# Two attention blocks on one core: a weight block loaded in two halves around the first key group, the last weight chunks in another order, a shorter head-by-head finish, and more products ahead of the first scores

## The chip, the cores and the metric

The kernel runs on one core of one Trainium2 chip. The metric is the device time of one execution in microseconds. Each comparison gives the median of the runs of a kernel, and a ratio to the kernel before, run on the same chip in the same rounds, with a 95% interval. The span of a profile was 1.7 to 1.9 us shorter than the device time of the same run.

## The reference

Two independent problems, A and B, of the same shape; their outputs are put side by side in the last dimension.

```python
B, Sq, D = 16, 32, 1024;  Hq, Hkv, Sk, Dh = 32, 4, 512, 128      # all bfloat16
q = (x @ wq).reshape(B, Sq, Hq, Dh).transpose(0, 2, 1, 3)
k, v = repeat(k_cache, 8, axis=1), repeat(v_cache, 8, axis=1)
p = softmax(einsum("bhqd,bhkd->bhqk", q, k) * Dh ** -0.5)
o = einsum("bhqk,bhkd->bhqd", p, v)
y = o.transpose(0, 2, 1, 3).reshape(B, Sq, Hq * Dh) @ wo          # (16, 32, 1024)
```

## The kernel before

The contraction of the q projection has 8 chunks of 128 (`DC = 8`, `HC = 4`). The first eight heads of A are projected chunk by chunk while their weights arrive (`w0`, `first_heads`). Everything after that is one long stream of products of 512 columns (the other projections, then the output projections). 128 attention slots are woven into it: each has four score matmuls, one exponential on ScalarE, sums on VectorE and, five slots later, four value matmuls. The loads go through one queue, that of the sync engine; in the trace of before, the loads from chunk 4 (landed at 10.35 us) to the first V group (29.98 us) landed in the order of their issue.

```python
            load_x(0, 0, TT // 2)                  # input, transposed later on TensorE
            load_w0(0, 1, 0, NF // 2)              # weights: chunk 0, heads 0 to 2
            load_x(0, TT // 2, TT)
            load_w0(0, 1, NF // 2, NF)             # chunk 0, heads 3 to 5
            load_w0(1, 2, 0, NF)                   # chunk 1
            load_x(2, 0, TT)
            load_w0(2, 3, 0, NF)
            load_w0(3, 4, 0, NF)
            load_w0(0, HC, NF, REP)                # chunks 0 to 3, heads 6 and 7
            load_w0(HC, HC + 1, 0, REP)            # chunk 4, all eight heads
            load_x_transposed(HC)                  # input chunks 4 and 5, transposed by DMA
            load_w0(HC + 1, HC + 2, 0, REP)        # chunk 5
            load_w0(HC + 2, DC, 0, REP)            # chunks 6 and 7
            load_x_transposed(HC + 2)              # input chunks 6 and 7
            load_wq(0, 2)                          # third weight block: heads 8 to 11, 1 MB
            load_k(0)                              # first K group, four transposed loads of 128 KB
            load_wq(0, 3)
            load_k(1)
            load_v(0)                              # first V group, 512 KB
            # ... (cut)
            warm_up(22)                            # 26 matmuls on constants in all
            # ... (cut: chunks 0 to 3)
            first_heads(range(REP), range(HC, DC - 2))
            for n, h in enumerate((0, 2, 4, 1, 5, 3, 6, 7)):
                first_heads((h,), (DC - 2, DC - 1))
                copy = nc.vector.tensor_copy if n % 2 else nc.scalar.copy
                copy(out=qT[0, 0][:, :, h, :], in_=first_q[h].rearrange("p (b s) -> p b s", s=SQ))
            # ... (cut)
            units = stream()
            run(units, 5)                          # five products of head 8 ahead of the first scores
            # ... (cut: plan of the later loads)
            for i in range(total_slots + LAG):
                if live:
                    do_loads(i)
                    scores(i)
                run(units, 1)
                # ... (cut: sums)
                if i >= LAG:
                    values(i - LAG)
                # ... (cut)
                run(units, 5)
                # ... (cut)
                run(units, 1 - (i % 4 == 3))
```

## Time and profile before

| | before |
|---|---|
| device time, median of 3 runs | 343.95 us (343.72 to 345.05) |
| span of the profiled run | 342.3 us |
| PE busy | 99% |
| PE start to start, 512 columns, full rate | 0.216 us |
| wait before the third weight block | 0.38 us |
| first product of chunk 4 to last matmul | 326.25 us |

The last row is worked out from the start times of the matmuls in the trace (12.682 us and 338.933 us).

The busy times of the engines, from the page of the kernel before (PE is TensorE's matmuls, PEld its weight loads, DVE VectorE, ACT ScalarE, POOL GpSimd; us, share of the span, instructions):

```profile
PE 337.9 (99%) x2128; PEld 214.1 (63%) x2128; DVE 266.2 (78%) x336; ACT 185.9 (54%) x209; POOL 46.7 (14%) x206
```

The waits of PE's weight loads between 5 and 60 us, kernel before (engine, line, what it waited for: us in total, times, longest us):

```profile
PEld L533 <- DMA w_sb<-in_A_wq_dram: 0.8, 2, 0.6
PEld L302 <- DMA wq_sb<-in_A_wq_dram: 0.7, 1, 0.7
PEld L523 <- DMA x_sb<-in_A_x_dram: 0.2, 1, 0.2
```

The timeline of the kernel before around the first scores (start, duration, engine, line, operation, output and inputs, count; in brackets the idle time before and what ended it; a row holds only what falls into the window that was asked for):

```profile
18.08 1.67 PE L533 MATMUL q_ps<-xT,w_sb 128*128 128x512 bf16 x7
...
19.79 0.69 DVE L561 CAST qT<-q_ps 128x512 bf16<-128x512 f32 x1 [0.17 <-PE q_ps L533]
...
19.96 0.76 PEld L302 LDWEIGHTS <-wq_sb 128*128 128x128 bf16 x5 [0.71 <-DMA wq_sb<-in_A_wq_dram]
19.97 1.25 PE L302 MATMUL q_ps<-xT,wq_sb 128*128 128x512 bf16 x5 [0.21 <-ACT qT L561]
...
21.05 0.60 PE L358 MATMUL s_ps<-qT,kT 128*128 128x256 bf16 x4
```

PE is the bound. What can be won without removing matmuls is the time in which PE stands still. The last matmul of the first eight heads starts at 19.372 us and the next is due 0.216 us later, at 19.59; it starts at 19.97. Two waits stand on this gap: the weight load waits for the third block (DMA), and the matmul is put down to a copy of ScalarE. The load landed at 19.92 us.

### The profile page before, as it was taken

What the parts mean: (1) busy time and instruction counts of PE and PEld (TensorE: products, weight loads), DVE (VectorE), ACT (ScalarE), POOL (GpSimd) and SP (SyncE); (2) the same over time, 40 slices, a digit from 0 to 9 for tenths busy, and PEclk for the clock granted to TensorE, in tenths of its full rate; (3) what the DMA queues carried; (4) which work ended last, traced back from release to release, by engine and by line L of the source; (5) the groups of instructions that cost most, each with busy time, mean ns of one, the idle gap of its engine ahead of it and who ended that gap; (6) DMA issues with size and microseconds to landing.
All of it is one profiled execution on the core that took longest, in us unless ns stands there. A gap on an engine that the chain in (4) does not pass through costs nothing.

```text
span 342.3 us, 5511 instructions
## 1 busy us (share of the span) xinstructions
PE 337.9 (99%) x2128; PEld 214.1 (63%) x2128; DVE 266.2 (78%) x336; ACT 185.9 (54%) x209; POOL 46.7 (14%) x206
## 2 busy tenths in 40 slices
PE   8999999999999999999999999999999999999996
PEld 6456666666666666666666666666666666666555
DVE  1057988888889888988888888888988888888540
ACT  3067666676676666666655455455455445555010
POOL 0001111100111111111101112222122110111100
PEclk9999999999999999999999999999999999999999
DMA  6999999999999999899999957999349995440001
GB/s 184 278 230 193 280 272 238 262 245 239 224 230 271 216 255 241 240 259 273 320 307 231 265 124 192 309 292 236 106 114 289 349 191 139 100 116 0 17 17 33
DMA packets 127088, 71.70 MB, mean 209 GB/s; under 512 B 75859, under 2 KB 126291, under 8 KB 127059
## 3 DMA queue, kind: packets, MB, share of 16 engines
q1 hardware_dynamic: 126528, 70.21, 86.0%
q0 software_dynamic: 384, 1.05, 1.2%
q8 instruction: 17, 0.28, 0.3%
q14 instruction: 15, 0.10, 0.1%
q10 hardware_dynamic: 144, 0.07, 0.1%
HBM read 50.86 MB, written 2.10 MB: 155 GB/s over the span
## 4 chain that ended last, share of the span: by engine, by line
PE 96%; DMA 1%; SPq 1%; ACT 0%; issue 0%; ACTq 0%
PE f_ps L321 32%; PE q_ps L302 28%; PE ob L426 16%; PE s_ps L358 16%; PE q_ps L533 3%; DMA w_sb<-in_A_wq_dram 1%; SPq L478 0%; SPq L466 0%; ACT qT L561 0%; ACT o_sb L330 0%; SPq L706 0%; ACTq L330 0%
## 5 line engine op out<-in xcount | busy, mean ns | idle before, releaser
L366 ACT ACTIVATE p_sb<-s_ps,shift 128x1024 bf16<-128x1024 f32 x128 | 142.6, 1114 | 100.5 <-PE s_ps L358 82.6
L377 DVE TRANSPOSE_TENSOR_REDUCE parts<-p_sb 128x32 f32<-128x1024 bf16 x128 | 158.8, 1241 | 20.0 <-ACT p_sb L366 18.3
L321 PE MATMUL f_ps<-wo_sb,oT 128*128 128x512 bf16 (+1 forms) x544 | 131.8, 367 | 0.0
L302 PE MATMUL q_ps<-xT,wq_sb 128*128 128x512 bf16 x448 | 117.6, 379 | 0.2 <-ACT qT L561 0.2
L426 PE MATMUL ob<-p_sb,v_sb 128*128 128x256 bf16 x512 | 76.8, 273 | 0.0
L358 PE MATMUL s_ps<-qT,kT 128*128 128x256 bf16 x512 | 76.8, 273 | 0.0
L321 PEld LDWEIGHTS <-oT 128*128 128x128 bf16 x544 | 53.2, 98 | 36.0
L358 PEld LDWEIGHTS <-kT 128*128 128x128 bf16 x512 | 56.9, 113 | 28.3
L302 PEld LDWEIGHTS <-wq_sb 128*128 128x128 bf16 x448 | 43.7, 98 | 32.0 <-DMA wq_sb<-in_A_wq_dram 0.7
L426 PEld LDWEIGHTS <-v_sb 128*128 128x128 bf16 x512 | 50.1, 98 | 20.0
L448 DVE TENSOR_TENSOR oT<-r,ob 128x512 bf16<-128x512 f32 x64 | 44.0, 687 | 22.6 <-PE ob L426 22.1
L412 DVE STREAM_TRANSPOSE r<-rall 128x512 f32<-128x512 f32 x64 | 44.2, 691 | 1.1
L310 ACT CAST qT<-q_ps 128x512 bf16<-128x512 f32 x56 | 32.6, 583 | 13.8 <-PE q_ps L302 13.8
L395 POOL COPY half<-cs 64x32 f32<-64x32 f32 x32 | 6.5, 204 | 228.4 <-DVE cs L385 228.4
L330 ACT CAST o_sb<-f_ps 128x512 bf16<-128x512 f32 (+1 forms) x17 | 9.5, 559 | 24.4 <-PE f_ps L321 16.7
L533 PE MATMUL q_ps<-xT,w_sb 128*128 128x512 bf16 (+1 forms) x70 | 15.1, 366 | 0.1
L385 DVE TENSOR_REDUCE cs<-parts 128x32 f32<-128x128 f32 x32 | 12.1, 377 | 1.1
L407 DVE RECIPROCAL rall<-sums 128x32 f32<-128x32 f32 x32 | 10.2, 318 | 1.6 <-POOL sums L404 1.6
L533 PEld LDWEIGHTS <-w_sb 128*128 128x128 bf16 x70 | 6.7, 99 | 7.2 <-DMA w_sb<-in_A_wq_dram 0.8
L561 DVE CAST qT<-q_ps 128x512 bf16<-128x512 f32 x4 | 2.8, 691 | 9.7 <-PE q_ps L533 9.6
L332 POOL DMA_DIRECT2D out_dram<-o_sb x8 | 4.6, 574 | 33.2 <-ACT o_sb L330 33.1
L396 POOL TENSOR_TENSOR half<-half,cs 64x32 f32<-64x32 f32 x32 | 7.8, 243 | 2.6
(25 smaller groups left out, 46.5 us busy)
## 6 DMA issues: line engine op xcount, KB each, us to landing
v_sb<-in_A_v_cache_dram SPq DMA_DIRECT2D x16, 512.0 KB, 6.8
wq_sb<-in_B_wq_dram SPq DMA_DIRECT2D x8, 1024.0 KB, 6.1
wo_sb<-in_A_wo_dram SPq DMA_DIRECT2D x8, 1024.0 KB, 6.9
v_sb<-in_B_v_cache_dram SPq DMA_DIRECT2D x16, 512.0 KB, 4.6
wo_sb<-in_B_wo_dram SPq DMA_DIRECT2D x8, 1024.0 KB, 8.6
wq_sb<-in_A_wq_dram SPq DMA_DIRECT2D x6, 1024.0 KB, 6.0
kT<-in_A_k_cache_dram SPq DMA_TRANSPOSE x64, 4.7
out_dram<-o_sb POOLq DMA_DIRECT2D x8, 128.0 KB, 4.2
```

The source lines that it names most:

```text
L302: nc.tensor.matmul(ps[:], lhsT=w[:, dc, (h % 4) * DH:(h % 4 + 1) * DH], rhs=xT[pr][:, dc, :], start=(dc == 0), stop=(dc == DC - 1),)
L310: nc.scalar.copy(out=qT[pr, g][:, :, hl, :], in_=ps[:].rearrange("p (b s) -> p b s", s=SQ),)
L321: nc.tensor.matmul(ps[:, 0:width], lhsT=oT[pr, tt][:, h, :], rhs=wo_tiles[pr, nh, h // REP][:, h % REP, off:off + width], start=(h == 0), ...
L358: nc.tensor.matmul(s_ps[:, c, :], lhsT=kT[:, i % GRP, c, :], rhs=qT[pr, g][:, b, :, :].rearrange("p h s -> p (h s)"), start=True, stop=True,)
L366: nc.scalar.activation(out=p_sb[:], in_=s_ps[:], func=ACTF.Exp, bias=shift[:], scale=SCALE)
L377: nc.vector.tensor_reduce(out=parts[k][:, q, :, :].rearrange("p c h -> p (c h)"), in_=st[i]["p"][:].rearrange("p c (h s) -> p (c h) s", s=SQ),
L385: nc.vector.tensor_reduce(out=cs[:], in_=parts.pop(k)[:].rearrange("p q c h -> p q h c"), axis=AX.X, op=ALU.add,)
L407: nc.vector.reciprocal(out=rall[:, k, :], in_=quad.pop(k)[:])
L412: nc.vector.transpose(out=r[:].rearrange("p n s -> p (n s)"), in_=rall[:, k, o * 2 * REP:(o + 1) * 2 * REP] .unsqueeze(2).to_broadcast([P, ...
L426: nc.tensor.matmul(ob[j][:, q, :], lhsT=v_sb[:, i % GRP, c, :], rhs=st[i]["p"][:, c, :], start=(c == 0), stop=(c == KC - 1),)
L448: nc.vector.tensor_tensor(out=out, in0=rcp.pop(j)[:].rearrange("p (q h) s -> p q h s", h=REP), in1=ob.pop(j)[:].rearrange("p q (h s) -> p ...
L533: nc.tensor.matmul(first_q[h][:, ts], lhsT=w0[dc // HC][:, dc % HC, h * DH:(h + 1) * DH], rhs=xT[0][:, dc, ts], start=(dc == 0 and t0 == 0 ...
```

## The change

Its intent is to take this gap away. The third block is loaded in two halves of two heads, one ahead of the first K group and one behind it. The last weight chunks come in another order. Only chunk 7 is finished head by head (before, chunks 6 and 7), which puts the eight copies closer together, so eight products of head 8 (before, five) are put ahead of the first scores to cover them. The input of B comes in two later loads instead of three, and some later weight loads are issued a slot earlier.

```diff
-            def load_wq(pr, c4, eng=None, parts=((0, 4),)):
+            def load_wq(pr, c4, a=0, b=4):          # loads heads a to b of a block of four
 ...
             load_x_transposed(HC)
-            load_w0(HC + 1, HC + 2, 0, REP)
-            load_w0(HC + 2, DC, 0, REP)
+            load_w0(HC + 1, DC - 1, 0, REP)
             load_x_transposed(HC + 2)
-            load_wq(0, 2)
+            load_w0(DC - 1, DC, 0, REP)
+            load_wq(0, 2, 0, 2)
             load_k(0)
+            load_wq(0, 2, 2, 4)
             load_wq(0, 3)
 ...
-            first_heads(range(REP), range(HC, DC - 2))
-            for n, h in enumerate((0, 2, 4, 1, 5, 3, 6, 7)):
-                first_heads((h,), (DC - 2, DC - 1))
+            first_heads(range(REP), range(HC, DC - 1))
+            for n, h in enumerate((0, 2, 4, 6, 5, 7, 1, 3)):
+                first_heads((h,), (DC - 1,))
 ...
-            run(units, 5)
+            run(units, DC)
 ...
-                need = ((c4 - 2) * 4 * DC - 5) / 6.75
+                need = ((c4 - 2) * 4 - 1) * DC / 6.75
 ...
-            for n, (d0, d1) in enumerate(((0, 2), (2, 5), (5, DC))):
-                at(GRP * (n + 3) - 2, load_xT_b, d0, d1)
+            for n in range(2):
+                at(GRP * (n + 3) - 2, load_xT_b, n * HC, (n + 1) * HC)
```

More of the change, by code (lines that the diff above doesn't have):

```diff
@@ L240, in fast_path @@
             wq_tiles, wo_tiles, k_tiles, v_tiles = {}, {}, {}, {}
-            def load_wq(pr, c4, eng=None, parts=((0, 4),)):
-                t = blk_tile([P, DC, 4 * DH], "wq_sb")
+            def load_wq(pr, c4, a=0, b=4):
+                if a == 0:
+                    wq_tiles[pr, c4] = blk_tile([P, DC, 4 * DH], "wq_sb")
                 v = problems[pr][3].rearrange("(c p) n -> p c n", p=P)
-                for a, b in parts:
-                    (eng or nc.sync).dma_start(
-                        out=t[:, :, a * DH:b * DH],
-                        in_=v[:, :, (c4 * 4 + a) * DH:(c4 * 4 + b) * DH],
-                    )
-                wq_tiles[pr, c4] = t
+                nc.sync.dma_start(
+                    out=wq_tiles[pr, c4][:, :, a * DH:b * DH],
+                    in_=v[:, :, (c4 * 4 + a) * DH:(c4 * 4 + b) * DH],
+                )
             def load_wo(pr, nh, hg):
```

## The prediction

> **What bounds the kernel.** TensorE. The page has PE busy 99% of a 342.3 us span at clock 1.0, and the chain of waits is 96% PE. In steady state one slot repeats every 2.385 us, and 512-column matmuls start 0.216 us apart [...]. Summing the matmuls after 4.06 us at these rates gives about 332.5 us of the 335.2 us up to the last one, so no reordering can win more than a little. The waits on PE and its weight loads show where it stands still: 0.29 us before chunk 2 (8.06 to 8.35, weights landing at 8.31), and 0.38 us before the first product of the third weight block (previous one due to end at 19.59, next starts 19.97; its 1 MB load landed at 19.92). Between 20 and 339 us PE waits for nothing on record.
>
> **What the change does.** No matmul, copy or byte is added or removed.
> 1. The third weight block is split: the half for heads 8 and 9 (512 KB) ahead of the first K group, the rest behind it. Loads land one after the other at about 250 to 285 GB/s here, so the first half should land about 2 us earlier, near 17.7 to 18 us, and the first K groups near 18.5 to 20 instead of 20.4 to 22.0. The 0.38 us gap goes. The second half should land near 22 and is needed near 24.
> 2. Chunk 5 now loads together with chunk 6 (512 KB): it lands about 1 us later, near 13.4, and is needed at 14.4. Chunk 7 lands near 15.5, needed at 17.9. No new wait expected.
> 3. Only chunk 7 is finished head by head, so eight products take 1.73 us instead of 3.45, and the eight copies to SBUF bunch up. VectorE's four copies of 0.69 us start near 18.5 and end near 21.1 to 21.3 (before: 20.48). The first scores need all eight. The eight products of head 8 (1.73 us, before only five) fill this time: scores are due at 21.3. It just fits; I allow 0.05 us, at worst 0.2, of new wait.
> 4. The stream is three products ahead: three fewer in the tail (0.65 us), three more in front: neutral. The B input comes in two transposed loads instead of three and some weight loads issue a slot earlier; both have slack.
>
> **Net.** 0.38 us removed, about 0.05 to 0.1 added: 0.3 us, all on the critical path, 0.1% of the span. The 0.29 us gap before chunk 2 stays.
>
> **Predicted time:** 343.65 us, 8 in 10 between 343.1 and 344.3. The runs of before spread from 343.72 to 345.05, more than the effect. Chances: faster by over 2% 0.005, within 2% 0.99, slower 0.005.
>
> **What would show it.** Right: no weight-load wait on the third block's load; first product of head 8 starts near 19.6, first scores near 21.3 to 21.45 with eight products ahead (before, 21.055 with five, which equals 21.70 with eight); the tail's run of output products is three shorter; span near 342.0. Step 3 wrong: PE or its sequencer waits for the VectorE copy before the first scores by over 0.2 us. Step 2 wrong: a wait for weights at 14.4 or 16.1.
>
> **What would make it wrong.** Split loads with 512-byte rows being slower, the second half or the first values' load arriving late (the latter's margin is 1.2 us now), the transposed loads' slow issue (1.3 to 3.8 us each on the queue) delaying what is behind them, or a shift of three products making ScalarE or VectorE late in some slot of the steady state, which repeats 128 times.

## The result, and the profile after

| | before | after |
|---|---|---|
| device time, median of 6 runs each | 344.01 us (343.72 to 345.05) | 343.94 us (343.29 to 344.54) |
| span of the profiled run | 342.3 us | 342.1 us |
| wait before the third weight block | 0.38 us | none |
| first product of chunk 4 | 12.68 us | 12.88 us |
| first product of chunk 4 to last matmul | 326.25 us | 325.86 us |

The ratio is 0.9991, with an interval from 0.9974 to 1.0008. A ratio is the mean time of one kernel's fast runs over that of the other's in the same rounds, so it is not quite the ratio of the medians above. The interval holds 1: the times do not show a gain.

The busy times of the changed kernel, from its page:

```profile
PE 338.1 (99%) x2128; PEld 214.6 (63%) x2128; DVE 265.6 (78%) x336; ACT 185.7 (54%) x209; POOL 46.6 (14%) x206
```

The view of the waits of PE lists one entry for the whole of the changed kernel, the start of the program. That of its weight loads between 5 and 60 us has none. The timeline around the first scores:

```profile
18.05 1.89 PE L533 MATMUL q_ps<-xT,w_sb 128*128 128x512 bf16 x8
...
18.47 2.05 ACT L561 CAST qT<-q_ps 128x512 bf16<-128x512 f32 x4 [9.58 <-PE q_ps L533]
...
18.69 2.48 DVE L561 CAST qT<-q_ps 128x512 bf16<-128x512 f32 x4 [10.18 <-PE q_ps L533]
19.57 1.61 PEld L301 LDWEIGHTS <-wq_sb 128*128 128x128 bf16 x8
...
19.78 1.89 PE L301 MATMUL q_ps<-xT,wq_sb 128*128 128x512 bf16 x8
21.29 0.55 PEld L357 LDWEIGHTS <-kT 128*128 128x128 bf16 x4
21.51 0.60 PE L357 MATMUL s_ps<-qT,kT 128*128 128x256 bf16 x4
```

The PE rows now follow one another without brackets. The bracket on the copies is idle time of ScalarE and VectorE, which cost PE nothing here: VectorE's four copies end at 21.17 us (18.69 + 2.48) and the scores start at 21.51, when they were due. The same matmul after the scores starts 0.387 us earlier, counted from chunk 4, and this difference stays the same to within 0.01 us to the end of the kernel. The tail shows the three products moved to the front, with the chain of waits of the kernel before first:

```profile
325.53 13.69 PE f_ps L321 x95
```

and that of the changed kernel:

```profile
325.98 13.04 PE f_ps L320 x92
```

But the span fell by only 0.2 us. The rest was lost before chunk 4, where both kernels issue the same loads and matmuls. The early PE rows of the timeline, kernel before, and the wait of its weight loads before chunk 2:

```profile
5.24 2.11 PE L533 MATMUL q_ps<-xT,w_sb 128*128 128x256 bf16 x13
7.18 0.61 PE L523 MATMUL xT_ps<-ident,x_sb 128*128 128x128 bf16 x8
...
8.35 10.91 PEld L533 LDWEIGHTS <-w_sb 128*128 128x128 bf16 x52 [0.62 <-DMA w_sb<-in_A_wq_dram]
```

and changed kernel:

```profile
5.25 2.58 PE L533 MATMUL q_ps<-xT,w_sb 128*128 128x256 bf16 x13
7.66 0.61 PE L523 MATMUL xT_ps<-ident,x_sb 128*128 128x128 bf16 x8
```

The same 13 matmuls took 0.47 us longer. In the trace the first 256-column matmuls start 0.213 us apart, and from some moment on 0.109 us apart. This moment was 5.2 us in the trace of before and 6.5 us in that of after. Matmuls of 128 columns show the switch too: they start 0.107 us apart before it and 0.056 us after it. It falls differently from run to run (3.7 to 7.0 us, table below); what sets its moment is not shown. The granted clock in these two profiles reads 1.00 all the time, so the switch has to be read from the start times. In the kernel before PE then stood 0.29 us for the weights of chunk 2, which landed at 8.31 us; in the changed kernel they landed at 7.54 us, and PE stood 0.02 us. So each trace has one early loss of its own, and the two partly cancel: chunk 4 starts 0.19 us later in the changed kernel, and 0.387 - 0.193 = 0.194 us is what its last matmul is early.

### The profile page after: what moved, and what is told of

The parts are those of the page before. It is cut to its first block, busy times and chain, and to the rows that moved or that the text cites. A ratio compares the mean times of both kernels' runs of the same rounds, so it can differ in the third digit from the quotient of the medians.

```text
span 342.1 us, 5510 instructions
## 1 busy us (share of the span) xinstructions
PE 338.1 (99%) x2128; PEld 214.6 (63%) x2128; DVE 265.6 (78%) x336; ACT 185.7 (54%) x209; POOL 46.6 (14%) x206
## 4 chain that ended last, share of the span: by engine, by line
PE 99%; ACT 0%; issue 0%; ACTq 0%
PE f_ps L320 32%; PE q_ps L301 28%; PE ob L425 16%; PE s_ps L357 16%; PE q_ps L533 4%; PE q_ps L515 1%; PE xT_ps L523 0%; ACT o_sb L329 0%; ACTq L329 0%
## 5 line engine op out<-in xcount | busy, mean ns | idle before, releaser
L309 ACT CAST qT<-q_ps 128x512 bf16<-128x512 f32 x56 | 32.6, 583 | 15.4 <-PE q_ps L301 15.4
L533 PE MATMUL q_ps<-xT,w_sb 128*128 128x512 bf16 (+1 forms) x70 | 15.4, 377 | 0.0
```

Source lines behind the costliest of these rows:

```text
L309: nc.scalar.copy(out=qT[pr, g][:, :, hl, :], in_=ps[:].rearrange("p (b s) -> p b s", s=SQ),)
L533: nc.tensor.matmul(first_q[h][:, ts], lhsT=w0[dc // HC][:, dc % HC, h * DH:(h + 1) * DH], rhs=xT[0][:, dc, ts], start=(dc == 0 and t0 == 0 ...
```

## The experiments

All twelve runs gave correct outputs. e11 is not in the table; its trace lacks records, and it is told in its section. The table collects the traces. "Full rate" is when the half rate ends, read from the start times to about 0.1 us. "Block" is the landing of the weights for the first product of the third block and when PE was due for it, "V" the same for the first V group; a wait is in brackets. "Interval" runs from the first product of chunk 4 to the last matmul.

| trace | full rate | chunk 4 | block landed / due | V landed / due | interval | ratio to before (95%) |
|---|---|---|---|---|---|---|
| before | 5.2 | 12.68 | 19.92 / 19.59 (0.38) | 29.98 / 31.23 | 326.25 | |
| after | 6.5 | 12.88 | 17.50 / 19.78 | 30.79 / 31.68 | 325.86 | 0.9991 (0.9974 to 1.0008) |
| e1_split_alone | 5.6 | 12.58 | 18.09 / 19.49 | 31.51 / 30.74 (0.81) | 326.70 | 1.0030 (1.0001 to 1.0058) |
| e2_whole_block | 7.0 | 13.12 | 18.69 / 20.02 | 28.81 / 31.93 | 325.86 | 1.0001 (0.9977 to 1.0025) |
| e3_five_ahead | 3.8 | 12.38 | 17.97 / 19.29 | 30.76 / 31.00 | 326.32 | 0.9999 (0.9976 to 1.0022) |
| e4_no_warm_up | 6.6 | 12.80 | 16.67 / 19.70 | 31.10 / 31.60 | 325.86 | 1.0031 (1.0006 to 1.0056) |
| e5_before_again | 5.2 | 12.29 | 19.39 / 19.20 (0.24) | 29.44 / 30.70 | 326.12 | 1.0001 (0.9984 to 1.0017) |
| e6_order_alone | 4.4 | 12.42 | 18.74 / 19.33 | 29.20 / 30.58 | 325.86 | 0.9999 (0.9982 to 1.0015) |
| e7_both_halves_first | 3.7 | 12.50 | 17.75 / 19.41 | 30.77 / 31.31 | 325.86 | one run |
| e8_after_again | 3.7 | 12.27 | 17.95 / 19.17 | 30.57 / 31.07 | 325.86 | 0.9992 (0.9975 to 1.0009) |
| e9_halves_by_chunk | 5.3 | 12.35 | 18.87 / 19.26 | 29.22 / 31.16 | 326.11 | one run |
| e10_two_queues | 4.2 | 12.59 | 18.12 / 19.50 | 28.86 / 30.75 | 325.86 | 1.0021 (1.0008 to 1.0035) |
| e12_after_third | 3.9 | 12.34 | 17.96 / 19.25 | 30.66 / 31.15 | 325.86 | 1.0010 (0.9997 to 1.0023) |

325.86 us is what the matmuls took in the traces whose views show no wait of PE after chunk 4 (after, e2 and e6 among them), so each trace says by itself how much it waited after chunk 4. Before chunk 4 the start varies from 12.27 to 13.12 us in kernels that issue the same loads and matmuls up to there (all but e4 and e10).

### e1_split_alone: the split without the rest

```diff
 kernel before (with the new load_wq of the change):
-            load_wq(0, 2)
+            load_wq(0, 2, 0, 2)
             load_k(0)
+            load_wq(0, 2, 2, 4)
```

> The kernel before with one part of the change: the third weight block in two halves around the first K group. Old head order, last two chunks head by head, five products ahead. Theory A (the late third block was the whole loss, the split is the whole gain): the first product of the third block starts 0.216 us after the last one of the first heads, the first scores follow five products (1.08 us) later without a wait, because the last copy ended 1.11 us after the last finishing product started and the scores are due 1.295 us after it. From the first product of chunk 4 to the last matmul: 325.86 us within 0.03, as in the changed kernel (326.25 before). Rival B (all three parts are needed): PE waits 0.1 us or more before the first scores, interval 325.95 or more. Rival C (PE waited for ScalarE's copy of head 4, as the waits on PE put it, not for weights): 0.2 us or more of gap stays before the third block.

The block was there in time (18.09 us, due at 19.49) and the first scores did not wait, with the old head order and five products ahead. So the split alone also closes the gap. But the kernel was slower, by 0.3%: its four runs took 344.21 to 345.56 us, against a median of 343.70 us for the kernel before on the same chip. The timeline at the first values:

```profile
30.53 0.38 PE L301 MATMUL q_ps<-xT,wq_sb 128*128 128x512 bf16 x1
...
31.55 0.33 PEld L425 LDWEIGHTS <-v_sb 128*128 128x128 bf16 x4 [1.03 <-DMA v_sb<-in_A_v_cache_dram]
31.55 0.61 PE L425 MATMUL ob<-p_sb,v_sb 128*128 128x256 bf16 x4 [0.65 <-DMA v_sb<-in_A_v_cache_dram]
```

The first V group landed at 31.51 us, 1.53 us later than in the trace of before, and PE stood still for 0.81 us. Theory A is right about the gap and wrong about the interval; none of the three had this. The split costs time in the loads behind it. This trace also ends later for another reason, not looked into: 3.79 us pass from the start of the last matmul to the end of the span, 3.35 to 3.42 us in the other traces. So the 0.3% is not all the wait for V.

### e2_whole_block: the rest without the split

```diff
 changed kernel:
-            load_wq(0, 2, 0, 2)
+            load_wq(0, 2)
             load_k(0)
-            load_wq(0, 2, 2, 4)
```

> The changed kernel with the third block loaded whole (1 MB) ahead of the first K group, all else as changed. Theory A: the block lands near 19.5 to 19.9 us and its first product is due at 19.6 to 19.8, so PE stands 0.1 to 0.35 us there; interval from the first product of chunk 4 to the last matmul 325.97 to 326.25 us. Rival C (the copy of head 4, now in another order): no gap, 325.86.

There was no gap. The whole block landed at 18.69 us, ahead of any time at which PE could ask for it in these traces, and V landed 2 us earlier than in the changed kernel. Theory A, by which the split is needed for the gain, falls. Two explanations were left: the copy of head 4 (rival C), or the new order of the last weight chunks, which this kernel also has.

### e3_five_ahead: the shorter finish without the eight products

```diff
 changed kernel:
-            run(units, DC)
+            run(units, 5)
```

> The changed kernel with five products ahead of the first scores in place of eight. VectorE's last copy ends 1.60 us after the last finishing product starts; the scores are due 0.216 + 1.08 = 1.295 us after it. Theory: PE waits 0.3 to 0.4 us before the first scores, interval from chunk 4 to the last matmul 326.17 to 326.27 us, so head by head over one chunk alone would give the gain back, and the eight products only pay for it. Rival: the number of products ahead does not matter, 325.86.

The timeline at the first scores:

```profile
18.19 2.48 DVE L561 CAST qT<-q_ps 128x512 bf16<-128x512 f32 x4 [10.18 <-PE q_ps L533]
...
19.28 1.24 PE L301 MATMUL q_ps<-xT,wq_sb 128*128 128x512 bf16 x5
...
20.82 0.60 PE L357 MATMUL s_ps<-qT,kT 128*128 128x256 bf16 x4 [0.30 <-DVE qT L561]
```

The scores were due at 20.36 us and started at 20.82, when VectorE's last copy (18.19 + 2.48 = 20.67) had been seen: 0.46 us, a little more than expected, and the interval is longer by the same. So the shorter finish loses 0.46 us alone, and the eight products only make up for it. The bracket shows 0.30 because the view ends the five products at 20.52 us (19.28 + 1.24), later than the scores were due; start times give the true wait.

### e4_no_warm_up: the first microseconds

```diff
 changed kernel:
-            warm_up(22)
             transpose_x(0, 0, TT // 2)
-            warm_up(3)
 ...
-            warm_up(1)
```

> The changed kernel without its 26 warm-up matmuls. In the traces of before and after the matmuls run at half rate (256 columns every 0.213 us) until about 5.1 us and about 6.4 us, and then at full rate (0.109 us). Theory: the onset [...]differs from run to run with the same instructions, which is where the two profiles differ by 0.48 us early on. Expected: [...] first product of chunk 4 0.5 to 2.2 us later than 12.88, span 0.5 to 2.2 us longer, time 344.4 to 346.1. Rival: in this stretch PE waits for weights anyway, the warm-ups do nothing: chunk 4 within 0.2 us of 12.7 to 12.9.

In the trace the full rate came at 6.6 us, 3.5 us after the first matmul of this kernel, and chunk 4 began at 12.80 us, as the rival had it. But its four spans are 342.0 (the profiled one), 342.6, 343.2 and 343.5 us and its ratio is 1.0031 with an interval above 1. The trace fell on the luckiest run. By the times the kernel without warm-ups is about a microsecond slower than the kernel before (0.31%, interval 0.06% to 0.56%); how that is made up is not shown by this one trace.

### e5_before_again and e6_order_alone: which part of the order matters

e5 is the kernel before, unchanged. e6 is:

```diff
 kernel before:
-            load_w0(HC + 1, HC + 2, 0, REP)
-            load_w0(HC + 2, DC, 0, REP)
+            load_w0(HC + 1, DC - 1, 0, REP)
             load_x_transposed(HC + 2)
+            load_w0(DC - 1, DC, 0, REP)
```

> The kernel before, unchanged, for a second trace and as a measure of the noise. Theory D (the late third block of before comes from its load order: the second transposed load of the input stands behind 768 KB of weights of the last three chunks, and in both traces with this order its packets stood still for about 0.9 us on all engines at 12.7 to 13.3 us, and in none of the four with the new order): such a stall again, the third block lands at 19.3 us or later, PE waits for it 0 to 0.4 us, interval from the first product of chunk 4 to the last matmul 325.87 to 326.3 us. Rival E (the first trace of before was a slow run by chance): the block lands near 18.7 us, no wait, 325.86. Ratio to before 1 within 0.3%.

> The kernel before with the new order of the last weight chunks alone (chunks 5 and 6 together, then the second transposed load of the input, then chunk 7); third block whole, old head order, five products ahead. Theory D: no stall near 13 us, the third block lands at 18.9 us or earlier, no wait at it nor at the first scores, first V group near 28.8 us, interval 325.86 us. If the split was needed: the block lands near 19.9, PE waits 0.2 us or more.

In e5 the block landed at 19.39 us and PE waited 0.24 us. The wait of its weight loads and the timeline of PE in e5:

```profile
PEld L302 <- DMA wq_sb<-in_A_wq_dram: 0.6, 1, 0.6
...
18.34 1.03 PE L533 MATMUL q_ps<-xT,w_sb 128*128 128x512 bf16 x4
19.44 1.25 PE L302 MATMUL q_ps<-xT,wq_sb 128*128 128x512 bf16 x5
```

and of e6:

```profile
18.03 1.46 PE L533 MATMUL q_ps<-xT,w_sb 128*128 128x512 bf16 x6
...
19.32 1.24 PE L302 MATMUL q_ps<-xT,wq_sb 128*128 128x512 bf16 x5
...
20.40 0.60 PE L358 MATMUL s_ps<-qT,kT 128*128 128x256 bf16 x4
```

In e6 the last product of the first heads starts at 19.109 us and the first of the third block 0.216 us later, with the old head order and the same copies. That rules out rival C: the matmul's wait put down to ScalarE was the weight load's, as the landing times say (19.92 and 19.97 us in before, 19.39 and 19.44 in e5). With two load lines replaced and nothing else the kernel reaches the interval of 325.86 us: no split, no eight products.

Why the block lands earlier is seen in part. The busy times by stretch (engines, then the granted clock, the DMA share and the GB/s moved, at the end of the line), kernel before:

```profile
12.00:13.00 1.00, 1.00 (x6) 0.49 (x5) 0.00 (x0) 0.00 (x0) 0.00 (x0) 1.00 1.00 344
13.00:14.00 1.00, 1.00 (x7) 0.41 (x5) 0.00 (x0) 0.00 (x0) 0.00 (x0) 1.00 1.41 109
14.00:15.00 1.00, 1.00 (x6) 0.47 (x5) 0.00 (x0) 0.00 (x0) 0.00 (x0) 1.00 0.99 244
```

and e6:

```profile
12.00:13.00 1.00, 1.00 (x6) 0.47 (x5) 0.00 (x0) 0.00 (x0) 0.00 (x0) 1.00 1.24 286
13.00:14.00 1.00, 1.00 (x7) 0.46 (x5) 0.00 (x0) 0.00 (x0) 0.00 (x0) 1.00 0.96 300
14.00:15.00 1.00, 1.00 (x6) 0.41 (x5) 0.00 (x0) 0.00 (x0) 0.00 (x0) 1.00 1.01 336
```

Between 13 and 14 us the three traces with the old order moved 109, 133 (e1) and 191 (e5) GB/s; ten of the eleven with the new order moved 279 to 358. The eleventh is e11 (below), which has the new order and another queue for one early load: it moved 173 GB/s, its packets stood still for about 1.2 us at 12.3 us, and its whole block landed at 19.87 us, as late as in before. The stall of packets that theory D named was there in before and e1, not in e5, and again in e11, so that part of the theory missed. The earlier landing with the new order thus rests on e2, e6 and e10 (18.12 to 18.74 us) against before and e5 (19.92 and 19.39 us), with e11 against it. What in the DMA engines delays the block stays open.

### e7_both_halves_first and e9_halves_by_chunk: what the split costs

```diff
 changed kernel, e7:
             load_wq(0, 2, 0, 2)
-            load_k(0)
             load_wq(0, 2, 2, 4)
+            load_k(0)
 changed kernel, e9 (the two halves are four chunks of the contraction each, all four heads):
-            load_wq(0, 2, 0, 2)
+            wq_tiles[0, 2] = blk_tile([P, DC, 4 * DH], "wq_sb")
+            for d0 in (0, HC):
+                nc.sync.dma_start(out=wq_tiles[0, 2][:, d0:d0 + HC, :],
+                                  in_=wq_v[:, d0:d0 + HC, 8 * DH:12 * DH])
             load_k(0)
-            load_wq(0, 2, 2, 4)
```

> The changed kernel with both halves of the third block ahead of the first K group. In the traces with the split the first V group landed at 30.7 to 31.5 us, with the whole block and the same order of the rest at 28.8. Theory F (the DMA engines run dry: transposed K loads take 1.26 us or more each to issue for 128 KB, with half as much data queued ahead the second half is issued only after them): V near 29.0 to 29.5 us, the rest being the 512-byte rows of the halves (a packet of 512 bytes takes 27 ns, one of 1024 bytes 46 ns). Rival G (the short rows or the extra load are the cost): V stays at 30.5 us or later. Either way no wait of PE after chunk 4, interval 325.86 us.

> The changed kernel with the third block in two loads again, both ahead of the first K group, but cut by chunks of the contraction: each half carries all four heads, so its rows stay 1024 bytes as in the whole block. With both halves of 512-byte rows ahead of K the first V group landed at 30.77 us, with the whole block at 28.81 and 29.20 us. Theory H (short rows make twice as many packets, and the transposed loads behind them are issued late [...]): V at 28.7 to 29.3 us. Rival I (one more load is what costs): V at 30.3 us or later. Block complete by 18.9 us, no wait of PE after chunk 4, interval from chunk 4 to the last matmul 325.86 us.

V landed at 30.77 us in e7, so theory F missed and rival G held. It landed at 29.22 us in e9, so theory H held in its number: two loads instead of one cost nothing, rows of 512 bytes in place of 1024 cost 1.5 us. These are one trace each, but the other traces agree: V landed at 30.57 to 31.51 us in the six others with rows of 512 bytes, and at 28.81 to 29.98 us in the six with the whole block (before, e2, e5, e6, e10, e11). In e7 the first transposed K load took 3.88 us to issue and the loads behind it came late: from 20 to 23 us the DMA engines moved 102 GB/s, in e9 234. The busy times by stretch of e7:

```profile
20.00:23.00 3.00, 3.00 (x18) 1.63 (x16) 0.83 (x3) 1.75 (x3) 0.00 (x0) 1.00 0.43 102
```

and of e9:

```profile
20.00:23.00 3.00, 3.00 (x18) 1.60 (x17) 0.83 (x3) 1.60 (x2) 0.00 (x0) 1.00 0.89 234
```

In e9 the first K load took 1.25 us to issue. Counted in the traces, 2550 data packets of earlier loads were still to start when this issue began in e7, and 2176 in e9. Over the fourteen traces more such packets went with a longer issue: 2268 to 2284 with 1.67 to 2.38 us, 2349 to 2357 (the old order) with 3.24 to 3.83 us. Whether the packets still to start hold the issue up is not shown: no run varied their number alone. e9 also showed what no theory had: at 186.8 us PE waited 0.22 us for a late K group of B, hence its interval of 326.11. The same group had 2.0 to 3.7 us to spare in the traces of before, after, e2, e6 and e8, so single late loads occur far from the change.

### e8_after_again and e12_after_third: the size of the effect

> The changed kernel, unchanged, for a second trace. Expected: interval from the first product of chunk 4 to the last matmul 325.86 us again, first V group lands 30.7 to 31.3 us with the first values due some 10.17 us after the first scores, a margin of 0.4 to 1.0 us; the start of chunk 4 moves with the onset of the full matmul rate, between 12.4 and 13.1 us. Ratio to before 0.998 to 1.001.

> The changed kernel, unchanged, in five rounds, for the size of its effect. Its two earlier comparisons gave 0.9991 and 0.9992, both with intervals that hold 1. Expected: ratio 0.9985 to 1.0005; interval from the first product of chunk 4 to the last matmul 325.86 us unless one of the late loads of this run is slow.

Both reached 325.86 us. In e12's trace 39 of the 2128 matmul records are missing, so its chunk 4 was counted one product further on. The margin of the first V group, 0.50 and 0.49 us, is less than half of the 1.25 us of before. The three ratios of the changed kernel are 0.9991, 0.9992 and 1.0010; e12's is above what was expected. All three intervals hold 1.

### e10_two_queues and e11_chunk1_on_act: tries to beat both

Both start from e6 and issue early weights on ScalarE's queue.

```diff
 e10:
+            load_x(0, 0, TT // 2)
+            load_w0(0, 1, 0, NF // 2, nc.scalar)
+            load_x(0, TT // 2, TT)
+            load_w0(0, 1, NF // 2, NF, nc.scalar)
+            load_w0(1, 2, 0, NF, nc.scalar)
             nc.scalar.preload_act_table_set("natural_log_exp_and_others")
-            load_x(0, 0, TT // 2)
-            load_w0(0, 1, 0, NF // 2)
-            load_x(0, TT // 2, TT)
-            load_w0(0, 1, NF // 2, NF)
-            load_w0(1, 2, 0, NF)
             load_x(2, 0, TT)
 e11:
-            load_w0(1, 2, 0, NF)
+            load_w0(1, 2, 0, NF, nc.scalar)
             load_x(2, 0, TT)
```

> A version meant to beat both: the kernel before with the new order of the last weight chunks, and the weights of chunks 0 and 1 issued on ScalarE's queue ahead of its table load, so that they do not wait behind the input's loads at 0.5 us each on the one queue. Where the full matmul rate came before 5.2 us, PE stood 0.1 to 0.6 us before chunk 1, whose weights landed near 6.2 us. Expected: chunk 1's weights land at 5.0 to 5.7 us, no wait before chunk 1, first product of chunk 4 at 11.9 to 12.9 us according to the onset of the full rate (before: 12.27 to 13.12), interval from there to the last matmul 325.86 us, span 341.1 to 342.3; ratio to before 0.997 to 1.000, so a gain of 0.1% that five rounds may not resolve. Rival: [...] the bytes only land in another order: chunk 4 not earlier than 12.3 us, or the input's first half later and the whole start with it.

> A second try at a version that beats both: the kernel before with the new order of the last weight chunks, and the weights of chunk 1 alone (192 KB) issued on ScalarE's queue after its table load, near 2.1 us in place of 2.84, so that the input's first quarter keeps its place and the loads behind it on the main queue are issued 0.5 us earlier. Expected: the input's first half lands near 3.25 us as before (3.75 with two queues from the start), chunk 1's weights at 5.3 to 5.9 us, no wait or under 0.2 us before chunk 1, first product of chunk 4 at 11.9 to 12.9 us, interval from there to the last matmul 325.86 us, ratio to before 0.997 to 1.000. Rival: [...] what lands earlier pushes the input of the first chunks later, and chunk 4 starts no earlier than 12.3 us, ratio 1.000 to 1.002.

In e10 the first half of the input landed at 3.75 us in place of 3.23 and the whole start moved with it; the rival held. e11 was slower by 0.56% (1.0043 to 1.0070): its load was issued at 0.85 us, while the table was still being loaded, not after it, and the first half of the input landed at 4.53 us, so this rival held too, with a larger loss than it said. The early PE rows of e11:

```profile
2.28 1.17 PE L515 MATMUL q_ps<-const-bfloat16-1.0 128*128 128x128 bf16 x9
4.58 0.61 PE L523 MATMUL xT_ps<-ident,x_sb 128*128 128x128 bf16 x4 [1.13 <-DMA x_sb<-in_A_x_dram]
4.98 0.52 PE L515 MATMUL q_ps<-const-bfloat16-1.0 128*128 128x128 bf16 x3
5.35 0.58 PE L533 MATMUL q_ps<-xT,w_sb 128*128 128x256 bf16 x2
```

PE stood for 1.13 us, and its matmuls ran at half rate until after 9 us; chunk 4 began near 15.4 us (this trace, too, lacks 39 records). In these two runs the second queue cost time: the critical first load landed 0.52 us (e10) and 1.30 us (e11) later than the 3.23 us of before. Why it did is not shown. No version beat both kernels.

## Why the prediction was right or wrong

The prediction was 343.65 us, between 343.1 and 344.3, and within 2% with a chance of 0.99. The median was 343.94 us. Point by point:

- **The bound and the size of what can be won**: right. PE is busy 99% in both traces, and the matmuls alone take 325.86 us from chunk 4 on in nine of the fourteen traces (the eight of the table, and that of e11 once its missing records are counted), with and without the split.
- **"The 0.38 us gap goes"**: right in the trace. The interval fell by 0.387 us, the gap and nothing else.
- **"0.05 to 0.1 added" for the copies**: measured 0.00. The copies ended at 21.17 us and the scores were due at 21.51. Without the eight products it would have been 0.46 (e3).
- **Step 1, the split as the cause of the gain**: enough, but not needed. The first half did land earlier, at 17.50 us (17.7 to 18 predicted), and the split alone closes the gap (e1). But a whole block in the new order lands at 18.69 and 18.74 us (e2, e6) and also in time. The prediction counted the order of the last chunks in step 2 only for the waits it might add. The second half landed at 23.15 us and was needed at 24.11 (22 and 24 foreseen); in e1 it had 0.12 us to spare.
- **Step 2, no new wait for chunks 5 to 7**: right. Chunks 5 and 6 landed at 12.69 us, chunk 7 at 15.16.
- **"The 0.29 us gap before chunk 2 stays"**: wrong. It is not a property of the kernel but a late load of one trace: the weights of chunk 2 landed at 8.31 us in before. In e5, the same kernel with the full rate at the same 5.2 us, they landed at 7.35 us, and PE stood 0.02 us, as in after. The full rate came between 3.7 and 7.0 us in the traces with the same early loads, and chunk 4 moved with it, from 12.27 us (full rate at 3.7 us, e8) to 13.12 us (7.0 us, e2), and with the weights of chunk 1, for which PE waited 0.23 us by the view of e3.
- **"Span near 342.0"**: 342.1 for the profiled run, 341.5 to 342.7 for its six. The onset of the full rate and the late loads moved a single run by more than the whole effect: chunk 4 by up to 0.85 us in the traces with the same early loads.
- **The risk named last, short rows and a thin margin of the first values' load**: real. The rows of 512 bytes cost 1.5 us of loading (e7 against e9), the margin fell from 1.25 us to 0.5 to 0.9, and where the eight products do not push the first values back, PE waits 0.81 us (e1).
- **The net of 0.3 us in the times**: not shown. The mean effect is smaller than the trace of before suggests, because that trace waited longer than the second trace of the same kernel did (0.38 and 0.24 us). A run without any wait after the earliest chunk 4 seen would have a span of 12.27 + 325.86 + 3.37 = 341.50 us, and 14 of the 34 runs of before that were timed with the experiments have spans of 341.5 or 341.6 us (the best of after: 341.4). So, by this estimate, many runs of the unchanged kernel hardly wait for the third block at all. The stated range of 343.1 to 344.3 us holds the time of the unchanged kernel too (344.01), so that the time fell into it is no evidence for the gain.

## What to carry to other kernels

When PE is busy 99% of the span, count the wait that a trace shows, and then count it again in a second trace of the same kernel before crediting it to a change: here it was 0.38 and 0.24 us, and the first 12 us moved by 0.85 us on their own. An interval between two fixed matmuls that leaves the start out told all the waits apart where times could not. Test the parts of a change one at a time, also the incidental ones: here the reordered loads (e6) or the split (e1) closed the gap alone, the split cost load time that the products ahead then hid, and the shorter finish and its eight products cancelled each other.

## What else the traces show of the start and of the loads

- The onset of the full rate: in e7 and e8 it came at 3.7 us, 2.8 us after the first matmul at 0.93 us; in e2 at 7.0 us, 6.1 us after it, with PE kept busy the whole time. The spread is 3.3 us.
- The time to issue a transposed load: one of 128 KB took at least 1.18 us, mostly 1.26 us, on the issuing queue, and up to 3.88 us (e7).
- The length of rows: packets of 512 bytes took 27 ns and packets of 1024 bytes 46 ns (medians in e7 and e9), so the longer ones moved 1.17 times as much in the same time. And behind two loads with rows of 512 bytes, ahead of transposed loads, the first V group landed 1.55 us later than behind two with rows of 1024 bytes (30.77 against 29.22 us, one trace each).
- The packets of a transposed load standing still together: in the changed kernel's trace 27 packets (20 of 256 bytes and 7 of 4) started between 15.85 and 15.89 us and took about 1.46 us each, where one of 256 bytes mostly takes 0.018 us. A stall of this kind, 1.4 to 2.1 us long, began between 15.6 and 18.4 us in thirteen of the fourteen traces; in e4 it fell at 26.0 us.
